# Two chunks of an activation matrix loaded by a transposing DMA instead of a plain load and eight TensorE transposes

## Chip, cores and metric

The kernel runs on one core of one Trainium2 chip. The metric is the device time of one execution in microseconds (us), as the median of several executions. Times of a trace count from the start of the program's span, which is about 1.8 us shorter than the device time.

## The reference

Two independent attention blocks, A and B, have the same shapes; their outputs are joined along the last axis.

```python
B, Sq, D = 16, 32, 1024;  Hq, Hkv, Sk, Dh = 32, 4, 512, 128      # all bf16
def block(x, k_cache, v_cache, wq, wo):
    q = (x @ wq).reshape(B, Sq, Hq, Dh).transpose(0, 2, 1, 3)
    k, v = (jnp.repeat(t, Hq // Hkv, axis=1) for t in (k_cache, v_cache))
    p = softmax(einsum("bhqd,bhkd->bhqk", q, k) * Dh ** -0.5)
    o = einsum("bhqk,bhkd->bhqd", p, v)
    return o.transpose(0, 2, 1, 3).reshape(B, Sq, Hq * Dh) @ wo
```

The first 20 us: the projection `x @ wq` of block A for its first eight heads. TensorE needs x with its 1,024 features on the partitions, as eight chunks of 128 features by 512 tokens. In memory x has tokens first, so each chunk must be transposed on the way.

## The kernel before

Chunks 0 to 3 of x are loaded plainly and transposed on TensorE. Chunks 4 to 7 come by a transposing load, two chunks at a time. `nc.sync` issues its loads one after another, in the order of the program; half of the first load of x goes out on ScalarE's queue. Here `P` is 128, `DC` is 8 (chunks), `TT` is 4 (token tiles), `HC` is 4, `REP` is 8 (heads), and `NF` is 6.

```python
            def load_x(d0, t0, t1, eng=nc.sync):            # two chunks, plain
                eng.dma_start(out=x_sb[:, t0:t1, d0 * P:(d0 + 2) * P],
                              in_=x_v[:, t0:t1, d0 * P:(d0 + 2) * P])
            def load_x_transposed(d0):                      # two chunks, transposing
                nc.sync.dma_start_transpose(out=xT[0][:, d0:d0 + 2, :],
                    in_=A_x.flatten_outer_dims()[:, d0 * P:(d0 + 2) * P])
            def load_w0(d0, d1, h0, h1):                    # weights: chunks d0..d1, heads h0..h1
                nc.sync.dma_start(out=w0[...], in_=wq_v[:, d0:d1, h0 * DH:h1 * DH])

            load_x(0, TT // 2, TT, nc.scalar)
            nc.scalar.preload_act_table_set("natural_log_exp_and_others")
            load_x(0, 0, TT // 2)
            load_w0(0, 1, 0, NF // 2)
            load_w0(0, 1, NF // 2, NF)
            load_w0(1, 2, 0, NF)
            load_x(2, 0, TT)                  # chunks 2 and 3
            load_w0(2, 3, 0, NF)              # weights of chunk 2, six heads, 192 KB
            load_w0(3, 4, 0, NF)              # weights of chunk 3
            load_w0(0, HC, NF, REP)
            load_w0(HC, HC + 1, 0, REP)
            load_x_transposed(HC)
            load_w0(HC + 1, DC - 1, 0, REP)
            load_x_transposed(HC + 2)
            load_w0(DC - 1, DC, 0, REP)
            # ... later blocks of wq, K and V ...

            warm_up(22)                       # matmuls on constants until x is there
            # ... transposes of chunks 0 and 1 ...
            for ts in ((0, TT // 2), (TT // 2, TT)):
                first_heads(range(0, NF // 2), (0,), *ts)   # six 256-column matmuls
            first_heads(range(NF // 2, NF), (0,))           # three of 512 columns
            first_heads(range(0, NF - 2), (1,))
            transpose_x(2, 0, TT, nc.vector.tensor_copy)    # four transposes, one copy
            transpose_x(3, 0, TT, nc.scalar.copy)
            first_heads(range(NF - 2, NF), (1,))
            first_heads(range(NF), (2, 3))
            # ... heads 6 and 7, then chunks 4 to 7 ...
```

## Time and profile before

| | before |
|---|---|
| median of the first 3 executions | 343.14 us (342.83 to 343.26) |
| span of the profiled one | 341.2 us |
| TensorE busy | 335.2 us, 98% |
| first matmul of chunk 2 | 7.69 us |
| first matmul of the ninth head | 18.91 us |

The first lines are from the profile page of the kernel before: its span, the busy time of each engine, the chain of work that ended last (shares of the span), and two groups of instructions (count, then busy us and mean ns of one, then idle time before them).

```profile
span 341.2 us, 5454 instructions
PE 335.2 (98%) x2082; PEld 213.6 (63%) x2121; DVE 265.5 (78%) x336; ACT 185.9 (54%) x209; POOL 46.7 (14%) x206
...
PE 98%; issue 1%; ACT 0%; ACTq 0%
...
L534 PE MATMUL q_ps<-xT,w_sb 128*128 128x512 bf16 (+1 forms) x65 | 14.4, 379 | 0.1
...
L534 PEld LDWEIGHTS <-w_sb 128*128 128x128 bf16 x67 | 6.8, 102 | 7.0 <-DMA w_sb<-in_A_wq_dram 0.2
```

TensorE (PE) bounds the kernel from end to end; any time won or lost on it at the start stays to the end, unless a later wait swallows it. There are 67 weight loads (PEld) for the first eight heads but only 65 matmuls, and each matmul has one weight load. Two matmul records are missing from this trace; that will matter.

The timeline of TensorE's matmuls (start us, duration us, line, what, count):

```profile
4.17 2.79 PE L534 MATMUL q_ps<-xT,w_sb 128*128 128x256 bf16 x13
6.79 0.61 PE L524 MATMUL xT_ps<-ident,x_sb 128*128 128x128 bf16 x8
7.45 11.62 PE L534 MATMUL q_ps<-xT,w_sb 128*128 128x512 bf16 x52
18.91 1.03 PE L301 MATMUL q_ps<-xT,wq_sb 128*128 128x512 bf16 x4
```

The second line holds the eight transposes that the change removes. A line ends when its last matmul ends, and matmuls overlap, so a cost on TensorE is read from starts, not from durations.

The timeline of SyncE's queue (SPq), where "us" is how long the issue held the queue:

```profile
2.21 0.43 SPq L477 DMA_DIRECT2D w_sb<-in_A_wq_dram  x1
2.69 0.43 SPq L465 DMA_DIRECT2D x_sb<-in_A_x_dram  x1
3.17 2.00 SPq L477 DMA_DIRECT2D w_sb<-in_A_wq_dram  x4
5.21 1.52 SPq L471 DMA_TRANSPOSE xT<-in_A_x_dram  x1
```

And the DMA view of the stretch 3.0 to 3.6 us (size of one, and us from the start of its issue to its landing):

```profile
x_sb<-in_A_x_dram SPq DMA_DIRECT2D x1, 256.0 KB, 3.9
w_sb<-in_A_wq_dram SPq DMA_DIRECT2D x1, 192.0 KB, 3.9
```

So the plain issue of x held the queue 0.43 us, the first transposing one 1.52 us (the second held it 2.64 us). Chunks 2 and 3 of x land at 6.55 us (2.69 + 3.86). The weights of chunk 2 land at 7.06 us (3.17 + 3.89), in time for 7.69 us.

### The profile page before, as it was taken

Reading aid. Unit: us, or ns where it says so; the run is one execution under the profiler, and the core shown is the slowest. Engines: PE = TensorE matmul, PEld = TensorE weight load, DVE = VectorE, ACT = ScalarE, POOL = GpSimd, SP = SyncE. Lnnn points to the kernel's source line nnn. Section 1 sums busy time; section 2 is a strip of 40 time slices with the busy share of each in tenths; the row PEclk is TensorE's granted clock in tenths of the full one; section 3 lists DMA queues with packets and bytes.
Section 4 is the critical chain, followed back from the end, with each engine's and each line's share of the span. In section 5 each row is a group of like instructions: output and inputs, shape, how many; then the busy total and the mean of one; then the engine's idle time right before and its main releaser. Section 6 shows DMA issues by size and latency. Waiting matters only on the chain.

```text
span 341.2 us, 5454 instructions
## 1 busy us (share of the span) xinstructions
PE 335.2 (98%) x2082; PEld 213.6 (63%) x2121; DVE 265.5 (78%) x336; ACT 185.9 (54%) x209; POOL 46.7 (14%) x206
## 2 busy tenths in 40 slices
PE   8999999999999999999999999999999999999996
PEld 6455666666666666666666666666666666666555
DVE  1046988888988898888888988879888888889540
ACT  3058666666667667666645545555555555555110
POOL 0001110011111111110012221222122101111100
PEclk9999999999999999999999999999999999999999
DMA  7999999999996987899999955998449997430001
GB/s 211 287 190 273 285 249 202 233 242 268 291 248 154 232 242 219 210 314 299 308 306 258 250 125 144 334 268 242 118 103 296 356 187 176 104 97 16 18 18 33
DMA packets 128094, 71.70 MB, mean 210 GB/s; under 512 B 75840, under 2 KB 127296, under 8 KB 128064
## 3 DMA queue, kind: packets, MB, share of 16 engines
q1 hardware_dynamic: 127264, 70.07, 84.1%
q0 software_dynamic: 384, 1.05, 0.9%
q8 instruction: 17, 0.28, 0.3%
q10 hardware_dynamic: 416, 0.20, 0.2%
q14 instruction: 13, 0.11, 0.1%
HBM read 50.86 MB, written 2.10 MB: 155 GB/s over the span
## 4 chain that ended last, share of the span: by engine, by line
PE 98%; issue 1%; ACT 0%; ACTq 0%
PE f_ps L320 32%; PE q_ps L301 28%; PE ob L425 17%; PE s_ps L357 16%; PE q_ps L534 4%; PE q_ps L516 1%; PE xT_ps L524 0%; ACT o_sb L329 0%; ACTq L329 0%
## 5 line engine op out<-in xcount | busy, mean ns | idle before, releaser
L365 ACT ACTIVATE p_sb<-s_ps,shift 128x1024 bf16<-128x1024 f32 x128 | 142.7, 1115 | 97.5 <-PE s_ps L357 88.1
L376 DVE TRANSPOSE_TENSOR_REDUCE parts<-p_sb 128x32 f32<-128x1024 bf16 x128 | 158.7, 1240 | 21.0 <-ACT p_sb L365 19.3
L320 PE MATMUL f_ps<-wo_sb,oT 128*128 128x512 bf16 (+1 forms) x525 | 128.2, 366 | 0.6
L301 PE MATMUL q_ps<-xT,wq_sb 128*128 128x512 bf16 x430 | 113.2, 379 | 0.5
L425 PE MATMUL ob<-p_sb,v_sb 128*128 128x256 bf16 x512 | 76.8, 273 | 0.8
L357 PE MATMUL s_ps<-qT,kT 128*128 128x256 bf16 x512 | 76.8, 273 | 0.0
L320 PEld LDWEIGHTS <-oT 128*128 128x128 bf16 x544 | 53.2, 98 | 35.3
L357 PEld LDWEIGHTS <-kT 128*128 128x128 bf16 x512 | 56.9, 113 | 28.3
L301 PEld LDWEIGHTS <-wq_sb 128*128 128x128 bf16 x448 | 43.8, 98 | 32.2
L425 PEld LDWEIGHTS <-v_sb 128*128 128x128 bf16 x512 | 50.1, 98 | 20.0
L447 DVE TENSOR_TENSOR oT<-r,ob 128x512 bf16<-128x512 f32 x64 | 43.9, 686 | 19.9 <-PE ob L425 19.4
L411 DVE STREAM_TRANSPOSE r<-rall 128x512 f32<-128x512 f32 x64 | 44.2, 691 | 1.1
L309 ACT CAST qT<-q_ps 128x512 bf16<-128x512 f32 x56 | 32.7, 583 | 16.5 <-PE q_ps L301 16.5
L394 POOL COPY half<-cs 64x32 f32<-64x32 f32 x32 | 6.5, 204 | 231.8 <-DVE cs L384 231.8
L329 ACT CAST o_sb<-f_ps 128x512 bf16<-128x512 f32 (+1 forms) x17 | 9.5, 559 | 23.6 <-PE f_ps L320 23.6
L534 PE MATMUL q_ps<-xT,w_sb 128*128 128x512 bf16 (+1 forms) x65 | 14.4, 379 | 0.1
L384 DVE TENSOR_REDUCE cs<-parts 128x32 f32<-128x128 f32 x32 | 12.1, 377 | 1.1
L406 DVE RECIPROCAL rall<-sums 128x32 f32<-128x32 f32 x32 | 10.2, 319 | 3.3 <-POOL sums L403 3.3
L534 PEld LDWEIGHTS <-w_sb 128*128 128x128 bf16 x67 | 6.8, 102 | 7.0 <-DMA w_sb<-in_A_wq_dram 0.2
L560 DVE CAST qT<-q_ps 128x512 bf16<-128x512 f32 x4 | 2.5, 684 | 10.2 <-PE q_ps L534 10.2
L331 POOL DMA_DIRECT2D out_dram<-o_sb x8 | 4.6, 574 | 29.3 <-ACT o_sb L329 29.3
L395 POOL TENSOR_TENSOR half<-half,cs 64x32 f32<-64x32 f32 x32 | 7.8, 243 | 2.6
(25 smaller groups left out, 44.7 us busy)
## 6 DMA issues: line engine op xcount, KB each, us to landing
v_sb<-in_A_v_cache_dram SPq DMA_DIRECT2D x16, 512.0 KB, 5.7
wq_sb<-in_B_wq_dram SPq DMA_DIRECT2D x8, 1024.0 KB, 5.7
wo_sb<-in_A_wo_dram SPq DMA_DIRECT2D x8, 1024.0 KB, 7.4
v_sb<-in_B_v_cache_dram SPq DMA_DIRECT2D x16, 512.0 KB, 4.7
wo_sb<-in_B_wo_dram SPq DMA_DIRECT2D x8, 1024.0 KB, 8.1
wq_sb<-in_A_wq_dram SPq DMA_DIRECT2D x5, 1024.0 KB, 5.8
wq_sb<-in_A_wq_dram SPq DMA_DIRECT2D x2, 512.0 KB, 6.7
kT<-in_A_k_cache_dram SPq DMA_TRANSPOSE x64, 4.4
```

Source lines behind the costliest of these rows:

```text
L301: nc.tensor.matmul(ps[:], lhsT=w[:, dc, (h % 4) * DH:(h % 4 + 1) * DH], rhs=xT[pr][:, dc, :], start=(dc == 0), stop=(dc == DC - 1),)
L309: nc.scalar.copy(out=qT[pr, g][:, :, hl, :], in_=ps[:].rearrange("p (b s) -> p b s", s=SQ),)
L320: nc.tensor.matmul(ps[:, 0:width], lhsT=oT[pr, tt][:, h, :], rhs=wo_tiles[pr, nh, h // REP][:, h % REP, off:off + width], start=(h == 0), ...
L357: nc.tensor.matmul(s_ps[:, c, :], lhsT=kT[:, i % GRP, c, :], rhs=qT[pr, g][:, b, :, :].rearrange("p h s -> p (h s)"), start=True, stop=True,)
L365: nc.scalar.activation(out=p_sb[:], in_=s_ps[:], func=ACTF.Exp, bias=shift[:], scale=SCALE)
L376: nc.vector.tensor_reduce(out=parts[k][:, q, :, :].rearrange("p c h -> p (c h)"), in_=st[i]["p"][:].rearrange("p c (h s) -> p (c h) s", s=SQ),
L384: nc.vector.tensor_reduce(out=cs[:], in_=parts.pop(k)[:].rearrange("p q c h -> p q h c"), axis=AX.X, op=ALU.add,)
L406: nc.vector.reciprocal(out=rall[:, k, :], in_=quad.pop(k)[:])
L411: nc.vector.transpose(out=r[:].rearrange("p n s -> p (n s)"), in_=rall[:, k, o * 2 * REP:(o + 1) * 2 * REP] .unsqueeze(2).to_broadcast([P, ...
L425: nc.tensor.matmul(ob[j][:, q, :], lhsT=v_sb[:, i % GRP, c, :], rhs=st[i]["p"][:, c, :], start=(c == 0), stop=(c == KC - 1),)
L447: nc.vector.tensor_tensor(out=out, in0=rcp.pop(j)[:].rearrange("p (q h) s -> p q h s", h=REP), in1=ob.pop(j)[:].rearrange("p q (h s) -> p ...
L534: nc.tensor.matmul(first_q[h][:, ts], lhsT=w0[dc // HC][:, dc % HC, h * DH:(h + 1) * DH], rhs=xT[0][:, dc, ts], start=(dc == 0 and t0 == 0 ...
```

## The change

The intent is to take eight transposes off TensorE, the bounding engine, and two copies off VectorE and ScalarE, by letting the DMA transpose chunks 2 and 3 as it already does for 4 to 7. (The smaller `x_sb` and the shorter signature of `load_x` are left out.)

```diff
-            load_x(2, 0, TT)
+            load_x_transposed(2)
             load_w0(2, 3, 0, NF)
             load_w0(3, 4, 0, NF)
@@
-            first_heads(range(0, NF - 2), (1,))
-            transpose_x(2, 0, TT, nc.vector.tensor_copy)
-            transpose_x(3, 0, TT, nc.scalar.copy)
-            first_heads(range(NF - 2, NF), (1,))
-            first_heads(range(NF), (2, 3))
+            first_heads(range(NF), (1, 2, 3))
```

More of the change, by code (lines that the diff above doesn't have):

```diff
@@ L456, in fast_path @@
             HC = DC // 2
-            x_sb = blk_tile([P, TT, HC * P], "x_sb")
+            x_sb = blk_tile([P, TT, 2 * P], "x_sb")
             xT[0] = blk_tile([P, DC, NTOK], "xT")
@@ L462, in fast_path, with load_x @@
             wq_v = A_wq.rearrange("(c p) n -> p c n", p=P)
-            def load_x(d0, t0, t1, eng=nc.sync):
-                eng.dma_start(
-                    out=x_sb[:, t0:t1, d0 * P:(d0 + 2) * P],
-                    in_=x_v[:, t0:t1, d0 * P:(d0 + 2) * P],
-                )
+            def load_x(t0, t1, eng=nc.sync):
+                eng.dma_start(out=x_sb[:, t0:t1, :], in_=x_v[:, t0:t1, 0:2 * P])
             def load_x_transposed(d0):
@@ L480, in load_w0 @@
                 )
-            load_x(0, TT // 2, TT, nc.scalar)
+            load_x(TT // 2, TT, nc.scalar)
             nc.scalar.preload_act_table_set("natural_log_exp_and_others")
-            load_x(0, 0, TT // 2)
+            load_x(0, TT // 2)
             load_w0(0, 1, 0, NF // 2)
```

## The prediction

> **What bounds the kernel.** The chain of work that ended last is 98% TensorE (the page's fourth part), and TensorE is busy 335.2 of 341.2 us (the first part). From 3.3 us on, it has no gap of half a microsecond in the timeline: 512-column matmuls start every 0.216 us. So only TensorE time can be won, and it keeps its worth only if nothing later makes TensorE wait.
>
> **What goes.** Eight TensorE transposes (from 6.79 us, one every 0.056 us) and two copies of 0.42 us (VectorE) and 0.59 us (ScalarE). The copies lie off the chain; the next matmul starts at 7.45 us where the rhythm would have put it at 6.79: 0.66 us off the chain, 0.19% of the span. The Trainium skill ("TensorE: Matmul & The Clock Gate", Part 4) gives about 275 ns for a transpose in a kernel; here the pitch is 56 ns, so less is saved than that suggests.
>
> **What comes.** A plain load of 256 KB (issued at 2.69 us, 0.43 us on SyncE's queue, landed at 6.55) becomes a transposing load. The two such loads of before held the queue 1.52 and 2.64 us and landed 5.8 us after their issue; the shortest of K held it 1.18 us. In an unfilled queue I take 1.5 us, so later issues move by about 1.1 us. A transposing load has 1,024 packets of 256 bytes, which in the second load of before went at 71 KB per 0.25 us, but in the first trickled over 2.2 us. The skill ("DMA: Bandwidth & Descriptors", Latency and other measured facts) gives 261 GB/s for a non-contiguous DMA transpose; the second load of before agrees (256 KB in about 1.0 us).
>
> **Where it meets the chain.** Without the transposes TensorE wants chunk 2 at 7.22 us (6.79 plus two matmuls). The weights of chunk 2 landed at 7.06 us after an issue at 3.17; issued at about 4.25 they land at about 7.4 to 8.0. The transposed x should land at about 6.5 to 8.0. So a new wait of 0.2 to 1.0 us just there, my middle 0.6. Next needs have slack: weights of chunk 3 (7.77, wanted over 1.3 us after chunk 2), heads 6 and 7 (9.13, wanted 10.5), chunks 4 and 5 of x (11.05, wanted 12.2), fourth block of wq (26.2, wanted about 27). The shift eats most of the third's slack, and may cost another 0.1. After that buffers coming free pace the loads, and the shift dies out.
>
> **Sum.** −0.66 + 0.6 + 0.1 = about 0. Predicted 343.2 us, range 342.3 to 344.1. Faster by over 2%: 0.5%; within 2%: 98.5%; slower by over 2%: 1%.
>
> **What would show it.** Right: TensorE's rows lose eight transposes; the issue of the transposing load on SyncE's queue is about 1.5 us long at 2.7 us; the timeline has an idle stretch of TensorE between 7.0 and 8.2 us before the chunk-2 matmuls, ended by a DMA (weights or x); the first matmul of the ninth head starts within 0.6 us of 18.91 us. Wrong: no wait at chunk 2 (then 0.6 us faster); or waits at chunk 4 to 7 or at the K and wq blocks around 22 to 27 us (then over 1 us slower).
>
> **What would make it wrong.** The first transposing load may have a start-up cost that now falls early (wait over 1 us), or, on the other side, the queue may be paced by the memory so that the longer issue hides. A clock disturbed by the gap would show as matmuls every 0.43 us.

## More of the kernel before

The chain of waits in its first 10 us (start us, us, what) is all TensorE:

```profile
0.93 2.52 PE q_ps L516 x22
3.45 0.92 PE xT_ps L524 x8
4.37 2.58 PE q_ps L534 x13
6.95 0.45 PE xT_ps L524 x8
7.40 0.05 issue
7.45 2.56 PE q_ps L534 x11
```

## The result and the profile after

| | before | after |
|---|---|---|
| median of 6 executions each | 343.20 us (342.83 to 343.48) | 343.65 us (343.43 to 344.07) |
| span of the profiled one | 341.2 us | 341.7 us |
| first matmul of chunk 2 | 7.69 us | 8.12 us |
| first matmul of the ninth head | 18.91 us | 19.35 us |
| start of ScalarE's last output copy | 338.22 us | 338.66 us |

The ratio is 1.0015, with a 95% interval of 1.0002 to 1.0028: the change costs about half a microsecond (0.07 to 0.96 us by the interval). Ratios here are the mean time of one kernel's fast runs over that of the other's in the same rounds, so they are not quite the ratios of the medians quoted. The last three rows of the table differ by 0.43, 0.44 and 0.44 us. Everything therefore happens before chunk 2; after that the two executions run in parallel.

The same lines of the page, of the kernel after (its line numbers are smaller by 3 in this part):

```profile
span 341.7 us, 5475 instructions
PE 336.4 (98%) x2113; PEld 213.1 (62%) x2113; DVE 265.1 (78%) x335; ACT 185.4 (54%) x208; POOL 46.7 (14%) x206
...
PE 97%; DMA 1%; SPq 1%; issue 0%; ACT 0%; ACTq 0%
...
L531 PE MATMUL q_ps<-xT,w_sb 128*128 128x512 bf16 (+1 forms) x67 | 14.2, 370 | 1.2 <-DMA w_sb<-in_A_wq_dram 1.2
```

The chain now has DMA and SyncE's queue in it, and TensorE was idle for 1.2 us before the matmuls of the first heads, ended by a load of weights. All 67 matmuls are recorded this time. (TensorE's busy time is higher although work was removed, because this trace lacks fewer records; it says nothing about the change.)

TensorE's timeline, kernel after:

```profile
4.09 2.81 PE L531 MATMUL q_ps<-xT,w_sb 128*128 128x256 bf16 x15
8.12 11.40 PE L531 MATMUL q_ps<-xT,w_sb 128*128 128x512 bf16 x52 [1.21 <-DMA w_sb<-in_A_wq_dram]
19.35 0.59 PE L301 MATMUL q_ps<-xT,wq_sb 128*128 128x512 bf16 x2
```

SyncE's queue, kernel after:

```profile
2.22 0.43 SPq L474 DMA_DIRECT2D w_sb<-in_A_wq_dram  x1
2.69 1.33 SPq L468 DMA_TRANSPOSE xT<-in_A_x_dram  x1
4.08 2.07 SPq L474 DMA_DIRECT2D w_sb<-in_A_wq_dram  x4
```

The DMA view of the stretch 4.25 to 4.5 us, kernel after, has the weights of chunk 2:

```profile
w_sb<-in_A_wq_dram SPq DMA_DIRECT2D x1, 192.0 KB, 4.0
```

They are issued at 4.08 us in place of 3.17 and land at 8.07 us in place of 7.06. The transposed x is not late at all: it lands at 6.36 us (2.69 + 3.67), earlier than the plain load in before.

The chain of waits in the first 10 us, kernel after, puts this together:

```profile
2.22 0.43 SPq L474
...
2.69 1.33 SPq L468
...
4.08 4.00 DMA w_sb<-in_A_wq_dram
...
8.12 1.90 PE q_ps L531 x8
```

Read from the bottom: the matmul at 8.12 us waited for the weights, the weights were on their way 4.00 us, and before that their issue stood behind the issue of the transposing load, which held the queue 1.33 us.

**What the transposes really cost.** In before, single starts in the trace are: last transpose 7.180 us, next recorded matmul 7.451 us. Transposes start every 0.056 us and 512-column matmuls every 0.216 us, and 7.180 + 0.056 + 0.216 = 7.452. So one of the two missing matmuls ran at about 7.236 us (the other fits the only double step of the rhythm, at 18.05 us), and the eight transposes cost TensorE 8 × 0.056 = 0.45 us, not the 0.66 us that the gap suggests. A later trace shows it directly: in e2 (below) no record is missing there, and the matmul starts at 8.888 us, 0.056 us after the last transpose at 8.832. The chunk-2 matmul of before came 0.239 us after the one ahead of it, 0.02 us more than the rhythm; that goes with the copies, for it needs the first of them.

**The account.** The thirteenth matmul of this stage started at 6.57 us in before and at 6.09 us in after: in that execution x landed 0.3 us earlier, and TensorE's matmuls reached their full rhythm (512 columns every 0.216 us; at half rhythm every 0.427 us, as e5 below shows) between 4.10 and 4.25 instead of between 5.02 and 5.17 us. The chunk-2 matmul came 1.593 us after the one ahead of it, 1.38 us more than the rhythm. So −0.48 (earlier start) − 0.45 (transposes) − 0.02 (wait for the copy) + 1.38 (wait) = +0.43 us, as measured.

### The profile page after: what moved, and what is told of

Read it like the earlier page. It is cut to its first block, busy times and chain, and to the rows that moved or that the text cites. A ratio compares the mean times of both kernels' runs of the same rounds, so it can differ in the third digit from the quotient of the medians.

```text
span 341.7 us, 5475 instructions
## 1 busy us (share of the span) xinstructions
PE 336.4 (98%) x2113; PEld 213.1 (62%) x2113; DVE 265.1 (78%) x335; ACT 185.4 (54%) x208; POOL 46.7 (14%) x206
## 4 chain that ended last, share of the span: by engine, by line
PE 97%; DMA 1%; SPq 1%; issue 0%; ACT 0%; ACTq 0%
PE f_ps L320 32%; PE q_ps L301 28%; PE ob L425 16%; PE s_ps L357 16%; PE q_ps L531 3%; DMA w_sb<-in_A_wq_dram 1%; SPq L468 0%; SPq L474 0%; SPq L465 0%; ACT o_sb L329 0%; ACTq L329 0%
## 5 line engine op out<-in xcount | busy, mean ns | idle before, releaser
L320 PE MATMUL f_ps<-wo_sb,oT 128*128 128x512 bf16 (+1 forms) x544 | 132.3, 366 | 0.0
L301 PE MATMUL q_ps<-xT,wq_sb 128*128 128x512 bf16 x448 | 116.9, 379 | 0.0
L309 ACT CAST qT<-q_ps 128x512 bf16<-128x512 f32 x56 | 32.7, 583 | 16.5 <-PE q_ps L301 16.5
L553 ACT CAST qT<-q_ps 128x512 bf16<-128x512 f32 x4 | 2.1, 599 | 13.3 <-PE q_ps L531 13.3
```

Of the source, the lines that this page charges most:

```text
L301: nc.tensor.matmul(ps[:], lhsT=w[:, dc, (h % 4) * DH:(h % 4 + 1) * DH], rhs=xT[pr][:, dc, :], start=(dc == 0), stop=(dc == DC - 1),)
L309: nc.scalar.copy(out=qT[pr, g][:, :, hl, :], in_=ps[:].rearrange("p (b s) -> p b s", s=SQ),)
L320: nc.tensor.matmul(ps[:, 0:width], lhsT=oT[pr, tt][:, h, :], rhs=wo_tiles[pr, nh, h // REP][:, h % REP, off:off + width], start=(h == 0), ...
```

## The experiments

Two theories were set against each other. **Theory I** (issue): the transposing load holds SyncE's queue 0.9 us longer, so what stands behind it is issued, and lands, that much later. **Theory D** (data): the transposing load moves its 256 KB in small packets that keep the DMA engines, so what is behind it in the stream is late whoever issues it. The windows view lends D some colour: from 5.5 to 6.5 us and from 6.5 to 7.5 us the DMA moved 350 and 256 GB/s in before but 240 and 210 GB/s in after, at about the same busy share (1.04 and 0.82; 1.03 and 0.89). The rows from 4.5 to 6.5 us, first of before, then of after; the last two numbers are the busy share of the DMA engines (overlapping packets make it more than 1) and GB/s:

```profile
4.50:5.50 1.00, 1.00 (x8) 0.66 (x7) 0.00 (x0) 0.28 (x1) 0.00 (x0) 1.00 1.00 316
5.50:6.50 1.00, 1.00 (x6) 0.48 (x5) 0.00 (x0) 0.00 (x0) 0.00 (x0) 1.00 1.04 350
...
4.50:5.50 1.00, 1.00 (x9) 0.56 (x7) 0.00 (x0) 0.21 (x1) 0.00 (x0) 1.00 1.21 230
5.50:6.50 1.00, 1.00 (x6) 0.44 (x5) 0.00 (x0) 0.00 (x0) 0.00 (x0) 1.00 1.03 240
```

The DMA view adds that from 4.6 to 5.4 us 670 of the 674 packets of after were under 512 bytes (17 of 391 in before). The DMA engines were full with them at a busy share of 1.24, and the packets of the chunk-2 weights came from about 5.5 us on, as the small ones ended. So after itself does not decide between the theories: the held queue and the full engines would both have kept these weights until about then.

All twelve runs were timed over five rounds. They were sent in four calls, each on its own chip with its own executions of the kernel before; so ratios are compared, not microseconds across calls.

| run | what it is | median us | before | ratio (95%) |
|---|---|---|---|---|
| e1 | after, weights early on ScalarE's queue | 343.25 | 343.34 | 1.0000 (0.9987 to 1.0013) |
| e2 | before, same move | 344.30 | 343.34 | 1.0035 (1.0016 to 1.0053) |
| e3 | before, plain load in three issues | 344.30 | 343.34 | 1.0024 (1.0011 to 1.0037) |
| e5 | plain load in place of the transposing one, wrong result | 342.95 | 343.34 | 0.9987 (0.9974 to 1.0000) |
| after again | unchanged | 343.77 | 343.52 | 1.0008 (0.9993 to 1.0023) |
| e6 | after, weights of chunk 2 first | 343.74 | 343.52 | 1.0007 (0.9992 to 1.0022) |
| e7 | e5 with the queue held | 344.45 | 343.52 | 1.0029 (1.0014 to 1.0044) |
| e8 | after, both weights first, one issue | 343.96 | 343.52 | 1.0019 (1.0005 to 1.0033) |
| e9 | after, weights later on ScalarE's queue | 344.61 | 343.47 | 1.0034 (1.0019 to 1.0048) |
| e10 | before, same move | 343.86 | 343.47 | 1.0012 (0.9998 to 1.0025) |
| e5 again | unchanged | 342.91 | 343.47 | 0.9983 (0.9969 to 0.9997) |
| e11 | before, 28 warm-up matmuls | 343.22 | 343.53 | 0.9995 (0.9982 to 1.0008) |

### e5: what the eight transposes are worth

```diff
-            load_x_transposed(2)
+            nc.sync.dma_start(
+                out=xT[0][:, 2:4, :].rearrange("p c (h d) -> p (c h) d", d=2 * P),
+                in_=x_v[:, :, 2 * P:4 * P],
+            )
```

This is the kernel after with the same bytes put untransposed where the transposed ones belong. Its output is wrong, which doesn't matter for the time. (The comparison with the reference with these inputs does not see two wrong chunks of x out of eight.)

> The kernel after with a plain load of the same 256 KB put straight into the place of the transposed chunks (wrong results on purpose): no TensorE transposes and no transposing load. It shows what the removal of the eight transposes is worth alone. From the trace of before, eight starts every 0.056 us are 0.45 us: theory I and D both expect 0.3 to 0.7 us faster than before (ratio 0.998 to 0.999), with the weights of chunk 2 landing near 7.0 us. If it is no faster than before, the transposes cost nothing and the wait at chunk 2 was there anyway.

Measured: 0.4 us faster than before by the medians, ratio 0.9987. The weights of chunk 2 landed at 7.20 us, 0.52 us after the x ahead of them, and TensorE waited for no DMA. In this trace the matmuls reached full rhythm only at 6.34 us. The run was repeated later:

> The plain load into the place of the transposed chunks once more (wrong results on purpose), on the same chip as the two others: what the eight TensorE transposes are worth when nothing replaces them. Expected 0.3 to 0.6 us faster than before (0.45 us from eight starts 0.056 us apart), less in a profile whose matmuls reach their full rhythm late.

Measured: 0.56 us faster by the medians, ratio 0.9983. Both fit the 0.45 us that eight starts of 0.056 us give, when nothing takes the place of the transposes. But the two intervals together reach from 0 to 0.31% (about 1 us), so the times alone would not tell 0.45 from the predicted 0.66 us; the starts do.

### e3 and e7: the queue held without a transposing load

e3 leaves the kernel before as it is, but issues the plain load of chunks 2 and 3 in three pieces:

```diff
-            load_x(2, 0, TT)
+            load_x(2, 0, 1)
+            load_x(2, 1, 2)
+            load_x(2, 2, TT)
```

> The kernel before, its plain load of chunks 2 and 3 of x split into three plain issues of the same bytes (about 1.4 us of SyncE's queue in place of 0.43), no transposing load added. Theory I: the weights of chunk 2 are issued about 0.95 us later (near 4.1 us), land near 8.0 us, and TensorE waits about 0.3 us for them (wanted at 7.7 us): 0.2 to 0.5 us slower than before, ratio 1.0006 to 1.0015. Theory D: same bytes in the same packets, so no change (ratio 0.9995 to 1.0005).

Measured: ratio 1.0024, about 1 us slower, twice the most that theory I expected. The weights of chunk 2 were issued at 4.12 us and landed at 8.46 us. But TensorE waited even before that, for the third piece of x, issued at 3.64 us. From the chain of waits of e3:

```profile
3.64 4.30 DMA x_sb<-in_A_x_dram
...
7.98 0.51 PE xT_ps L526 x6
```

No byte was added and no transposing load; three issues instead of one made the kernel slower than the change did.

e7 takes the fast but wrong e5 and puts two loads of 8 KB behind its plain load:

```diff
+            hold = const.tile([P, 2, 32], BF16, name="hold")
+            for k in range(2):
+                nc.sync.dma_start(out=hold[:, k, :], in_=x_v[:, k, 0:32])
             load_w0(2, 3, 0, NF)
             load_w0(3, 4, 0, NF)
```

> The kernel with the plain load in place of the transposing one (wrong results on purpose), and behind that load two plain loads of 8 KB each into an unused tile, which hold SyncE's queue for about the time that the transposing load held it (0.96 us more) and bring next to no data. Theory I: weights of chunk 2 issued at 4.1 us, landing near 8 us, TensorE waits about 0.5 to 1.4 us there, and the time is that of the kernel after within 0.3 us, 0.4 to 1.0 us more than without the two loads (342.95 us). Theory D: no transposing packets, so the weights land by 7.5 us and the time stays within 0.2 us of 342.95 us.

Measured: ratio 1.0029, against 0.9987 and 0.9983 without the two small loads: 0.42 to 0.46% or about 1.5 us, more than the 0.4 to 1.0 us that theory I expected. From the chain of waits of e7:

```profile
3.17 0.50 SPq L491
...
3.71 0.44 SPq L491
...
4.20 4.82 DMA w_sb<-in_A_wq_dram
...
9.06 1.04 PE q_ps L537 x4
```

The weights land at 9.02 us, later than in after, with not one transposing packet ahead of them. Part of the loss in that trace is something else: the weights of chunk 0 for heads 3 to 5, issued at 1.75 us as always, landed at 5.61 us (4.49 and 5.03 us in after and before), and TensorE waited 0.7 us for them. But the wait at chunk 2 was 1.3 us by itself (1.46 us beyond the rhythm). Theory D expected the time of e5. So transposing packets are not needed to make the weights this late; that they add nothing in after is not shown. e7 is not quite free of small packets either, as its two loads come in rows of 64 bytes.

The distance between the landing of chunks 2 and 3 of x and that of the weights of chunk 2 fits theory I. It grows with the distance between their issues, which was 0.48 us in before and e5, 1.38 us in after, and 1.51 us in e7:

| run | issues between the two | from x landed to weights landed, us |
|---|---|---|
| before; e5; e5 again | x plain, then weights | 0.51; 0.52; 0.53 |
| after; after again | x transposing, then weights | 1.71; 1.47 |
| e7 | x plain, two tiny loads, then weights | 2.04 |

### After, once more

> The kernel after once more, unchanged, for a second trace and for times on the same chip as the next three. Expected: ratio to before 1.0005 to 1.0025; weights of chunk 2 issued at 4.1 us and landing at 7.7 to 8.4 us; TensorE waits there 0.5 to 1.6 us, depending on when it got to chunk 2.

Measured: 343.77 us, ratio 1.0008, in the expected range; its interval includes 1. The transposing load held the queue 1.33 us again, the weights of chunk 2 were issued at 4.08 us and landed at 8.31 us, and the chunk-2 matmul at 8.36 us came 1.16 us later than the rhythm. The thirteenth matmul started at 6.55 us, as in before, so here the account is −0.02 − 0.45 − 0.02 + 1.16 = +0.67 us, as measured (8.36 − 7.69).

### e1, e2, e9, e10: issuing the weights from another queue

If the held queue is the trouble, the weights of chunks 2 and 3 can go out on ScalarE's queue. In e1 that is done with the kernel after, in e2 with the kernel before:

```diff
             nc.scalar.preload_act_table_set("natural_log_exp_and_others")
+            load_w0(2, 3, 0, NF, nc.scalar)
+            load_w0(3, 4, 0, NF, nc.scalar)
@@
-            load_w0(2, 3, 0, NF)
-            load_w0(3, 4, 0, NF)
```

> The kernel after, with the weights of chunks 2 and 3 issued from ScalarE's queue (at about 2.6 and 3.1 us) instead of behind the transposing load on SyncE's queue. Theory I (the issue of the transposing load holds SyncE's queue 1.33 us instead of 0.43, and the weights behind it are late by that): the weights of chunk 2 land at 6.2 to 7.2 us, TensorE's wait at chunk 2 shrinks from 1.2 us to at most 0.4, and the run is 0.3 to 0.9 us faster than the kernel before (ratio 0.997 to 0.999). Theory D (the 1,024 small packets of the transposing load keep the DMA engines, whoever issues the rest): the weights still land at 7.5 us or later, the wait stays at 0.8 us or more, the ratio to before is 1.000 to 1.002.

> The kernel before with the same move of the two weight loads to ScalarE's queue; a control. TensorE did not wait for these weights in before, so both theories expect no change: ratio 0.9990 to 1.0010, and no DMA wait of TensorE at chunk 2. If it is faster by 0.3 us or more, the gain of the first experiment is not owed to the held queue.

Both missed, for a reason in the design: ScalarE's sequencer did not wait for its table load, and the two issues went out at 1.34 and 1.83 us, among loads wanted sooner. In e1 the weights of chunk 2 landed at 5.04 us, but those of chunk 0, issued at 1.25 us, landed at 4.70 instead of 3.67 us, and TensorE waited for those instead. The control e2 shows the harm alone: 1 us slower, the weights of chunk 1 landing at 7.52 us instead of 5.75, and 1.2 us of waits for weights. The pair also shows something that neither expectation asked for. e1 and e2 differ from each other as after and before do, with no urgent weights behind the transposing load, and there the kernel with the transposing load was the faster one: 343.25 against 344.30 us. Why the plain load of e2 comes with later weights is not known.

So in e9 (kernel after) and e10 (kernel before) a one-column copy by ScalarE into the place to be loaded holds each issue back until the table load is over:

```diff
+            for d in (2, 3):
+                nc.scalar.copy(out=w0[0][:, d, 0:1], in_=warm[:, 0:1])
+                load_w0(d, d + 1, 0, NF, nc.scalar)
```

> The repair of the first experiment, whose loads from ScalarE's queue went out at 1.34 and 1.83 us and so pushed aside loads wanted earlier. Here a one-column copy on ScalarE into the place to be loaded makes each of the two issues wait until ScalarE's table load is over: weights of chunk 2 at about 2.9 us, of chunk 3 at about 3.4 us, past the transposing load that still holds SyncE's queue from 2.7 to 4.0 us. Theory I (the hold makes the weights late): weights of chunk 2 land at 6.3 to 7.3 us, chunk 3 by 8.2 us, TensorE's wait for a DMA at chunks 2 and 3 is under 0.5 us, and the run is 0.3 to 0.8 us faster than before (about that of the plain wrong load, and 0.5 to 1.2 us faster than after). Theory D (the transposing load's packets make them late): weights of chunk 2 land after 7.5 us, the wait is 0.8 us or more, and the time is that of after.

> The kernel before with the same late issues from ScalarE's queue, as a control. TensorE did not wait for these weights in before: both theories expect the time of before within 0.3 us (ratio 0.999 to 1.001). If it is faster by as much as the run with the transposing load, the gain there belongs to the move and not to the change.

Measured for e9: the issues went out at 2.83 and 3.45 us, and the weights of chunk 2 landed at 6.53 us, as theory I expected. But the run was not faster: ratio 1.0034. The wait had moved to the transposed x itself. From the chain of waits of e9:

```profile
2.69 6.48 DMA xT<-in_A_x_dram
...
9.21 0.81 PE q_ps L532 x3
```

Issued at 2.69 us as in after, it now took 6.48 us instead of 3.67. The control e10 was 1.0012, with two short waits (0.3 and 0.2 us by the waits view) for x and weights. This pair shows a cost of the transposing load that theory I does not have: x and the weights of chunks 2 and 3 were issued at the same times in both (2.69, 2.83 and 3.45 us), and all three had landed at 9.17 us with the transposing load but at 8.15 us with the plain one. It is not quite theory D either, for the weights of chunk 2 landed earlier with the transposing load (6.53 against 7.23 us); x itself was late. (In e1 and e2 it was the other way round: 7.46 and 8.31 us.) The Trainium skill says of this ("DMA: Bandwidth & Descriptors", Issuing engines are not separate DMA queues) that loads from any queue run on the same 16 DMA engines and interleave, and that a second queue saves only issue time. e1 and e9 agree with it: the issue time was saved, and other loads paid. In e9 x and the two weights were there at 9.17 us, no sooner than in after (8.99 us); in e1 they were there at 7.46 us, but the weights of chunk 0 came a microsecond late. Theory I fits the late weights of after; how much of their lateness is the held queue and how much the transposing packets stays open. That the loss can be had back by another queue was not shown: e1 came level with before, and e9 was slower.

### e6, e8: another order on the same queue

```diff
 e6:                                     e8:
+            load_w0(2, 3, 0, NF)       +            load_w0(2, 4, 0, NF)
             load_x_transposed(2)                    load_x_transposed(2)
-            load_w0(2, 3, 0, NF)       -            load_w0(2, 3, 0, NF)
             load_w0(3, 4, 0, NF)       -            load_w0(3, 4, 0, NF)
```

> The kernel after with one pair of issues swapped: the weights of chunk 2 ahead of the transposing load, those of chunk 3 still behind it. Theory I (the held queue delays what is behind it): the weights of chunk 2 are issued at 2.7 us and land near 6.3 us, the transposed x is issued at 3.2 us and lands at 6.9 to 7.4 us, so the wait at chunk 2 shrinks to 0 to 0.7 us and the run is 0.3 to 0.9 us faster than the kernel after. Theory D (the small packets of the transposing load themselves slow the stream): what was won at chunk 2 is lost at chunk 3 or later, and the run is within 0.2 us of the kernel after.

> The kernel after with the weights of chunks 2 and 3 in one issue, ahead of the transposing load: two holds of 0.43 us become one, and nothing urgent stands behind the transposing load. Theory I: weights land near 7.0 us, transposed x at 7.3 to 7.9 us, wait at chunk 2 0.2 to 1.0 us, later loads about 0.5 us earlier than in the kernel after; the run is 0.2 to 0.8 us faster than after, and perhaps level with or 0.3 us faster than before. Theory D: not faster than after by more than 0.2 us.

Measured for e6: landings came as theory I said (weights of chunk 2 at 6.20 us, transposed x at 7.27 us), and the chunk-2 matmul started at 7.31 us, 0.38 us before that of the kernel before. But the weights of chunk 3 now stood behind the held queue. From the chain of waits of e6:

```profile
3.17 1.33 SPq L468
...
4.55 4.51 DMA w_sb<-in_A_wq_dram
...
9.10 1.04 PE q_ps L531 x4
```

The first matmul of chunk 3 came at 9.10 us, half a microsecond behind the rhythm. Over five rounds e6 is level with after (343.74 and 343.77 us), not 0.3 to 0.9 us faster; by the time alone this is what theory D had expected. The lateness again falls on what stands behind the transposing load, which both theories allow.

In e8 the weights landed at 7.03 us and the transposed x at 8.08 us. No wait for a DMA is listed, because in this execution TensorE got to chunk 2 late: its matmuls reached full rhythm only at 6.65 us; the chunk-2 matmul started at 8.12 us, right after x, and 0.16 us later than the rhythm. The next load behind the transposing one landed 0.89 us after it, in time for heads 6 and 7. The ratio is 1.0019, no gain over after, where theory I expected 0.2 to 0.8 us. With x landing at 8.08 us, chunk 2 could not start before about 8.1 us however early TensorE got there, against 7.69 us in before.

### e11: the spread between executions

```diff
-            warm_up(22)
+            warm_up(28)
```

> About the spread between runs, which is as large as the effect: in the twelve traces read so far TensorE's matmuls went from half to full rhythm at anything from 3.75 to 6.65 us. The kernel before with 28 instead of 22 warm-up matmuls, so that TensorE has no gaps of 0.14 to 0.3 us at 3.1 to 3.8 us while x lands. If such gaps delay the full rhythm: full rhythm by 4.8 us at the latest, the five times within 0.5 us of each other, and the run 0 to 0.5 us faster than before. If they have nothing to do with it: the rhythm doubles late in some runs as before, the first real work starts about 0.6 us later, and the run is 0 to 0.6 us slower than before.

Measured: 343.22 us against 343.53, ratio 0.9995; the six times lie between 343.14 and 343.93 us. In its trace the transposes of x, ahead of the first real matmul, already run at full rhythm from 3.95 us on. That is as expected if the gaps delay the full rhythm, but it is inconclusive: five times lie within 0.23 us, one is as slow as the slow ones of before, the interval includes 1, and e8 reached full rhythm only at 6.65 us without any such gap. What decides the moment of full rhythm stays open. It matters for reading the other numbers: executions of the unchanged kernel before spread over 1.3 us within one call (342.8 to 344.13 us), more than the effect under study, and a microsecond at half rhythm is half a microsecond of work.

No correct kernel beat the kernel before beyond its interval.

## Why the prediction was right or wrong

The range (342.3 to 344.1 us) held 343.65 us, and "within 2%" was right, which was all but certain with 0.19% of the span at stake. The point, 343.2 us, was 0.45 us low, and its balance of "about 0" came out as a loss.

- **Mechanism: right where the trace shows it.** A held queue, late weights of chunk 2, one idle stretch of TensorE between 7.0 and 8.2 us ended by a DMA, the ninth head within 0.6 us of 18.91 us (19.35; in the second trace 19.59, 0.68 us off), parallel timelines after that. The chain of waits of after names exactly this, and e3 and e7 show that a held queue without a transposing load makes what stands behind it late. That the longer issue is the whole cause was assumed, and is not shown: in after the DMA engines were full with transposing packets in the same stretch, and e9 beside e10 lost time with the issues of these loads unchanged.
- **"0.66 us off the chain": too large.** It was 0.45 us. The gap from 6.79 to 7.45 us held a matmul whose record was missing. The page showed it: 67 weight loads for 65 matmuls. e5 (0.4 and 0.56 us) agrees, within wide intervals.
- **"A new wait of 0.2 to 1.0 us, my middle 0.6": too small.** It was 1.38 and 1.16 us beyond the rhythm. The shift of the issues was overrated (0.91 us, not 1.1), but the weights landed at 8.07 and 8.31 us, after the predicted 7.4 to 8.0. A wait over 1 us was foreseen only for a slow start of the transposing load, but x landed in time in both traces. In the first trace TensorE also reached chunk 2 0.48 us earlier than assumed, which the wait swallowed.
- **"May cost another 0.1": nothing.** The shift at chunk 2 (0.43 us) and at the ninth head (0.44 us) are the same; all later slack held.
- **The transposed x at 6.5 to 8.0 us: a little pessimistic.** It landed at 6.36 and 6.84 us and was never what TensorE waited for in after.

Open: how the lateness of the weights divides between the held queue and the transposing packets; why a load of 192 KB takes about 4 us or more to land in this phase at all (3.9 us in before, 4.0 and 4.2 us in the two traces of after, 4.8 us in e7); why the transposing load of e9 took 6.48 us; and what sets the moment of full rhythm.

## What to carry to other kernels

Taking work off the bounding engine pays only if what replaces it does not delay the next input of that engine: here 0.45 us of transposes was traded for a load whose issue held the queue 0.9 us longer, and the loss fell on the unrelated loads behind it. So when loads go out just in time from one queue, count the issue time of each as well as its bytes and packets, and follow the chain of waits back to the queue. Before sizing a gap in a trace, check that no record is missing, for instance by comparing the counts of weight loads and matmuls.

## What the Trainium skill lacked or had wrong

- "DMA: Bandwidth & Descriptors", Issuing engines are not separate DMA queues, calls the issue time on the sequencer "usually small relative to the DMA itself". Here a transposing load of 256 KB held SyncE's queue 1.33 us of its 3.67 us to landing, a plain one 0.43 of 3.86 us, and three plain issues in place of one made the kernel about 1 us slower.
- "TensorE: Matmul & The Clock Gate", Part 4: PE-mode transpose, gives about 275 ns for a 128×128 bf16 transpose in a kernel, as the duration of one. In before one between matmuls at full rhythm lasted 219 ns. What the part lacks is the time from start to start, which is what several in a row cost: 56 ns here, and 0.45 us for eight. (The prediction set the 275 ns beside this 56 ns as if they were one measure.)
- "TensorE: Matmul & The Clock Gate", Part 1: The HAM clock gate, puts the change to full rhythm around 4 us into sustained matmuls, ±500 ns between runs (it also calls the count of slow matmuls variable). Here matmuls began at 0.93 us, and in the traces before the last run it came at 3.75 to 6.65 us, which is 2.8 to 5.7 us in; up to the change there was no gap between matmuls in the two traces at the ends, e1 and e8. The profile's granted clock stood at 0.998 to 1.0 for the same executions, so it did not show the half-rhythm start.
